# Two heads to a task for half of the kept heads, with V in 8 KB rows, in a two-layer cached decode kernel

## The chip, the cores and the metric

One core of one Trainium2 chip runs the kernel. The metric is the device time of one execution in microseconds (us), the median over the runs of a measurement. The kernel before has 1160.96 us (three runs, 1160.77 to 1161.88).

## What is computed

Two layers of grouped-query attention against a cache and a dense block with SiLU, for 8 batches of one token. The same caches and weights serve both layers.

```python
B, Sq, D = 8, 1, 512
Hq, Hkv, Sk, Dh = 32, 8, 8192, 128          # 4 query heads to each cached head
k_cache, v_cache: (B, Hkv, Sk, Dh) bf16     # 2 MB for each batch and head
...
q = (x @ wq) by heads
scores = einsum("bhqd,bhkd->bhqk", q, k) * Dh ** -0.5
o = einsum("bhqk,bhkd->bhqd", softmax(scores), v)
attention = o @ wo
dense(x) = silu(x @ w1) @ w2                # F = 1792
...
x = x + attention(layernorm(x)); x = x + dense(layernorm(x))     # layer 0
x = x + attention(layernorm(x)); x = x + dense(layernorm(x))     # layer 1
```

## The kernel before

**Tasks and positions.** A task is one (layer, batch, head): 128 tasks in an order that `make_tasks` writes out. A task has eight positions, so that the loop over `p` runs over 1024 positions and some more at the end. A head's 8192 keys are four granules `k` of 512 KB (128 partitions of 4 KB). At each position the loop emits, in this order, what is due there: the task's queries (`emit_q`), DVE transposes of K (`emit_t`), scores (`emit_s`), the product with V (`emit_pv`), the steps that join and fold the output (`emit_own`, `emit_join`, `emit_fold`), the softmax of an earlier task, one stage of a batch's chain (wo, layer norm, the dense block, the queries of layer 1), and the loads (`issue_until`). Each engine runs its instructions in that order.

**Slots.** `ARENA` has 28 slots of 4 KB in each partition. Heads 3 to 7 of a batch are kept: their K (20 slots) is loaded and transposed in layer 0 and stays for layer 1. Heads 0 to 2 load K in both layers, one granule a slot. V is loaded in both layers, one granule a slot. Kept K is loaded 2 MB at a time, in rows of 16 KB; all other K and all V in rows of 4 KB. For each batch the order is: five kept tasks of layer 0, some five tasks of heads 0 to 2 of other batches or of layer 1 (in which the chain of the batch runs), then its five kept tasks of layer 1. In the middle part kept K fills 20 slots, and eight are left.

**Loads.** `plan_loads` sorts the loads by `need`, the position at which one is used, and gives each the slot that comes free first; `after` is the position after which it may be issued. SP issues them all in that order, and waits at each for the slot's last reader. V has `need = i0 + 1 + LP` for a granule that starts at position `i0`; `LP = 14` is the distance from scores to the product with V.

**Scores and softmax.** K is transposed in place by DVE in 32x32 blocks of 32-bit words (line 497). A kept head is scored at once (line 563), 16 matmuls of 512 columns that fill one PSUM bank `SCp`. The softmax of task `p // 8 - 1` follows: DVE's maximum over the bank (574) and `top` (576), POOL's maximum over partitions (579), DVE's shift (583, 586), ACT's exp into `P` (590), the row sums (597, 599), PE's transposes of `P` (608), ACT's copy to `PT` (612). `P` shares its bytes with `E`, where the output is joined (643, 651). PV is line 628, the last fold 665, the norm 675, a wo part 780.

```python
soft = {0: [softmax_max], 2: [softmax_shift, softmax_exp], 4: [softmax_sum], 5: [emit_pt], 7: [softmax_rcp]}
```

Of the kernel before, what the change touches and what calls it, by code (L numbers as in the profile page):

```python
# [5 lines left out]
HQ = 32  # L6
DH = 128
SM_SCALE = DH ** -0.5
# [11 lines left out]
READ = (1, 1, 1, 4, 4, 4, 4, 4)  # L20
KEEP = 20
LT = 1
PRE = 10
LP = 14
EARLY = 4
DEAL_AT = 30
WO_FROM = 36
NTP = 2
NSCP = 2
NPT = 1  # L30
# [12 lines left out]
NAT = 2  # L43
CW = 32
# [98 lines left out]
class Load:  # L143


    __slots__ = ("kind", "b", "g", "k", "turn", "need", "free", "slot", "after", "wide")

    def __init__(self, kind, b, g, k, need, free, wide=1):
        self.kind, self.b, self.g, self.k, self.turn = kind, b, g, k, k
        self.need, self.free, self.wide = need, free, wide  # L150
        self.slot, self.after = None, None


def make_tasks(nb, nkv, keep_from):
# [10 lines left out]
    na = 0  # L165
    for b in range(nb):
        if b:
            tasks += kept[b]
        size = -(-(2 * first * (nb - 1)) // nb) if b in (0, nb - 1) else 2 * first * (nb - 1) // nb
        must = max(0, first * min(b + 1, nb - 1) - na)  # L170
        nd = size if b == nb - 1 else min(len(behind), first, size - must)
        tasks += behind[:nd]
        del behind[:nd]
        take = ahead[na:na + size - nd]
        na += len(take)
        tasks += take
        if b + 1 == nb:
            tasks += behind
        tasks += c[b]
        behind += d[b]  # L180
# [4 lines left out]
def plan_loads(tasks, kept, nslot, ngran):  # L185

    at = {t: i for i, t in enumerate(tasks)}
    loads = []
    for i, (layer, b, g) in enumerate(tasks):
        for k in range(ngran):  # L190
# [8 lines left out]
            loads.append(Load("V", b, g, k, i0 + GPG - 1 + LP, i0 + GPG - 1 + LP))  # L199
# [9 lines left out]
    for d in loads:  # L209
        w = ngran if d.kind == "K" and (d.g, d.k) in kept else 1  # L210
        if w > 1 and d.k:
            d.slot = whole[d.g] + d.k
            d.after = by
            assert d.after < d.need or d.need == -1 and d.after == -2, (d.kind, d.need, d.after)
            continue
# [7 lines left out]
        if w > 1:  # L223
            whole[d.g] = d.slot
# [19 lines left out]
def _build(ctx, nc, A_x, A_k_cache, A_v_cache, A_wq, A_wo, B_w1, B_w2, out):  # L244
# [43 lines left out]
    def half(slot, h):  # L288
# [8 lines left out]
    XT = [sb([128, KT, B], BF16, f"XT{n}") for n in range(3)]  # L297
# [5 lines left out]
    QT2 = [sb([128, HQ], BF16, "QT2") for _ in range(2)]  # L303
# [12 lines left out]
    hsT = sb([128, FT * B], BF16, "hsT")  # L316
    xnT = sb([128, KT, B], BF16, "xnT")
    s1 = sb([128, B], FP32, "s1")
    s1a = sb([128, B], FP32, "s1a")
    s2 = sb([128, 1], FP32, "s2")  # L320
    s2a = sb([128, 1], FP32, "s2a")
    top = sb([128, REP], FP32, "top")
    tops = sb([128, REP], FP32, "tops")
    ssm = [sb([128, REP], FP32, "ssm") for _ in range(NST)]
    ssa = [sb([128, REP], FP32, "ssa") for _ in range(NST)]
    widths = {"own_q": NQ, "hm": REP, "far": REP, "mine": REP, "own_x": XW, "real": 1, "rowmax": 1,
              "eps": 1, "shift": 1, "eh": FT, "vr": B, "yr": B, "tr": B}
    widths.update({f"rcp{n}": REP for n in range(NST)})
    widths.update({f"rs{n}": 1 for n in range(NST)})
    row = sb([128, sum(widths.values())], FP32, "row")  # L330
    tiny, at_col = {}, 0
    for name, w in widths.items():
        tiny[name] = row[:, at_col:at_col + w]
        at_col += w
    own_q, hm, far, mine, own_x, real, rowmax, eps, shift, vr, yr, tr = (
        tiny[n] for n in ("own_q", "hm", "far", "mine", "own_x", "real", "rowmax", "eps", "shift", "vr", "yr", "tr"))
    rcp = [tiny[f"rcp{n}"] for n in range(NST)]
    rs = [tiny[f"rs{n}"] for n in range(NST)]

# [56 lines left out]
    v_slot = {}  # L396

    def issue(d):
        cache = A_k_cache if d.kind == "K" else A_v_cache
        if d.kind == "K":  # L400
            src = cache[d.b, d.g].rearrange("(p k c) d -> k p (c d)", k=NGRAN // d.wide, p=128)[d.k // d.wide]
        else:
            src = cache[d.b, d.g].rearrange("(k p c) d -> k p (c d)", k=NGRAN, p=128)[d.k]
# [7 lines left out]
    with nc.Block() as block:  # L411

        @block.sync
        def _(sync_eng):
# [13 lines left out]
                    hm[:, :], lanes.rearrange("p c (k r) -> p r c k", k=NGRAN), AX.XY, ALU.add),  # L428
                reads=["ident"], writes=["hm"],
            )  # L430
            op(
# [7 lines left out]
            for n in range(NSCP):  # L439
                op(dve, lambda n=n: dve.memset(SCp[n][:, :], 0.0), writes=[f"SC{n}"])  # L440
            op(dve, lambda: dve.tensor_reduce(real[:, :], hm[:, :], AX.X, ALU.add), reads=["hm"], writes=["real"])
# [3 lines left out]
            op(dve, lambda: dve.tensor_scalar(  # L445
                far[:, :], hm[:, :], real[:, 0:1], FAR, op0=ALU.subtract, op1=ALU.mult),
               reads=["hm", "real"], writes=["far"])
# [57 lines left out]

            span_of = {}
# [10 lines left out]
            def emit_queries(layer, b):  # L517
                if layer == 0:
                    q, rq = QT1[:, b * HQ:(b + 1) * HQ], f"QT1_{b}"
                else:  # L520
                    q, rq = QT2[b % 2][:, :], f"QT2_{b % 2}"
# [9 lines left out]
            def emit_q(ti):  # L531
                layer, b, g = tasks[ti]
                if ti == span_of[(layer, b)][0]:
                    emit_queries(layer, b)
                n = ti % NQB
                at = qset[(layer, b)] * NPART * HQ
                op(dve, lambda: dve.tensor_tensor(
                    QB[n][:, :, :].rearrange("p i (a r) -> p i a r", a=NQ),
                    QSp[:, at:at + NPART * HQ].rearrange("p (i h) -> p i h", h=HQ)[:, :, g * REP:(g + 1) * REP].unsqueeze(2)
                    .to_broadcast([128, NPART, NQ, REP]),  # L540
                    own_q[:, :].unsqueeze(1).unsqueeze(3).to_broadcast([128, NPART, NQ, REP]), ALU.mult),
                   reads=["QS", "own_q"], writes=[f"QB{n}"])

            def emit_s(i):
# [9 lines left out]
                bank, qn = ti % NSCP, ti % NQB  # L554
# [17 lines left out]
            def softmax_max(ti):  # L572
                bank = ti % NSCP
                op(dve, lambda: dve.tensor_reduce(rowmax[:, :], SCp[bank][:, :], AX.X, ALU.max),  # L574
                   reads=[f"SC{bank}"], writes=["rowmax"])
                op(dve, lambda: dve.scalar_tensor_tensor(  # L576
                    top[:, :], hm[:, :], rowmax[:, 0:1], far[:, :], op0=ALU.mult, op1=ALU.add),
                   reads=["hm", "rowmax", "far"], writes=["top"])
                op(pool, lambda: pool.partition_all_reduce(tops[:, :], top[:, :], 128, bass.bass_isa.ReduceOp.max),  # L579
                   reads=["top"], writes=["tops"])  # L580

            def softmax_shift(ti):
                op(dve, lambda: dve.scalar_tensor_tensor(  # L583
                    mine[:, :], tops[:, :], -SM_SCALE, hm[:, :], op0=ALU.mult, op1=ALU.mult),
                   reads=["tops", "hm"], writes=["mine"])
                op(dve, lambda: dve.tensor_reduce(shift[:, :], mine[:, :], AX.X, ALU.add), reads=["mine"], writes=["shift"])  # L586

            def softmax_exp(ti):
                bank, st = ti % NSCP, ti % NST
                op(act, lambda: act.activation(  # L590
                    P[:, :].rearrange("p (x j k) -> p k x j", x=CPB, k=NGRAN),
                    SCp[bank][:, :].rearrange("p (k x j) -> p k x j", k=NGRAN, x=CPB), ACT.Exp, bias=shift[:, 0:1], scale=SM_SCALE, accum_out=rs[st][:, :]),
                   reads=[f"SC{bank}", "shift"], writes=["P", f"rs{st}"])

            def softmax_sum(ti):
                st = ti % NST
                op(act, lambda: act.activation(ssm[st][:, :], hm[:, :], ACT.Copy, scale=rs[st][:, 0:1]),  # L597
                   reads=["hm", f"rs{st}"], writes=[f"ssm{st}"])
                op(pool, lambda: pool.partition_all_reduce(ssa[st][:, :], ssm[st][:, :], 128, bass.bass_isa.ReduceOp.add),  # L599
                   reads=[f"ssm{st}"], writes=[f"ssa{st}"])  # L600

            def emit_pt(ti):
                pb = ti % NPT
# [494 lines left out]
```

## Time and profile before

| | |
|---|---|
| median of three runs | 1160.96 us (1160.77 to 1161.88) |
| the profiled execution | 1160.11 us, span 1158.0 us |
| busy share of the span | PE 61%, DVE 64%, ACT 29%, POOL 10% |
| granted TensorE clock | 0.605 of full speed |
| HBM read | 465.05 MB, 402 GB/s over the span |
| chain that ended last | DMA 52%, DVE 20%, issue 10%, PE 8%, SP's queue 5%, ACT 4% |
| loads of V | 512 of 512 KB, 10.7 us from issue to landing (median) |
| loads of K | 192 of 512 KB, 8.2 us; 40 of 2 MB, 19.1 us |

The page cuts the span in 40 slices; for each it gives DMA's busy share in tenths and the GB/s. Stretches of time show the busy time of each engine, the granted clock, DMA's share (it exceeds 1 where packets overlap) and the rate. In the timeline a line is: start in us, duration, engine, line of the source, operation, output and input, count, and in brackets the idle time before it and what ended it. SPq is the queue from which SP issues loads.

### The profile page before, as it was taken

What the parts mean: (1) busy time and instruction counts of PE and PEld (TensorE: products, weight loads), DVE (VectorE), ACT (ScalarE), POOL (GpSimd) and SP (SyncE); (2) the same over time, 40 slices, a digit from 0 to 9 for tenths busy, and PEclk for the clock granted to TensorE, in tenths of its full rate; (3) what the DMA queues carried; (4) which work ended last, traced back from release to release, by engine and by line L of the source; (5) the groups of instructions that cost most, each with busy time, mean ns of one, the idle gap of its engine ahead of it and who ended that gap; (6) DMA issues with size and microseconds to landing.
All of it is one profiled execution on the core that took longest, in us unless ns stands there. A gap on an engine that the chain in (4) does not pass through costs nothing.

```text
span 1158.0 us, 26486 instructions
## 1 busy us (share of the span) xinstructions
PE 703.8 (61%) x10768; PEld 343.4 (30%) x10768; DVE 740.4 (64%) x1781; ACT 337.9 (29%) x764; POOL 117.1 (10%) x296
## 2 busy tenths in 40 slices
PE   1434666556755676567655587557655676557666
PEld 1212342223321342134322342124222342134233
DVE  3646773677557675677457664777467755677564
ACT  0442234223332233222422233222323233223332
POOL 0000111001110111001100111001100111001100
PEclk9756567565655566555855565566756565565665
DMA  9999999999999999999999999999999999999994
GB/s 372 393 411 415 407 409 413 416 406 409 408 420 413 398 407 417 418 395 408 410 416 414 403 407 416 419 397 409 412 419 403 407 408 418 415 403 407 407 408 192
DMA packets 112601, 466.80 MB, mean 403 GB/s; under 512 B 11984, under 2 KB 16096, under 8 KB 106720
## 3 DMA queue, kind: packets, MB, share of 16 engines
q1 hardware_dynamic: 112480, 465.11, 100.1%
q8 instruction: 85, 1.39, 0.5%
q14 instruction: 36, 0.29, 0.1%
HBM read 465.05 MB, written 0.01 MB: 402 GB/s over the span
## 4 chain that ended last, share of the span: by engine, by line
DMA 52%; DVE 20%; issue 10%; PE 8%; SPq 5%; ACT 4%; POOL 1%; DVEq 0%; ACTq 0%; POOLq 0%
DMA arena<-in_A_k_cache_dram 32%; DMA arena<-in_A_v_cache_dram 20%; DVE E L651 7%; DVE arena L497 7%; SPq L379 5%; DVE row L574 3%; PE SCp L563 2%; PE OTp L628 2%; PE TPp L608 2%; ACT E L590 2%; ACT PT L612 1%; DVE top L576 1%; POOL tops L579 1%; ACT E L643 1%; DVE row L586 1%
## 5 line engine op out<-in xcount | busy, mean ns | idle before, releaser
L497 DVE STREAM_TRANSPOSE arena<-arena 128x1024 int32<-128x1024 int32 x352 | 434.1, 1237 | 230.3 <-DMA arena<-in_A_k_cache_dram 230.0
L590 ACT ACTIVATE E<-SCp,row 128x512 bf16<-128x512 f32 x128 | 183.0, 1429 | 655.8 <-DVE row L586 620.5
L628 PE MATMUL OTp<-arena,PT 128*16 128x512 bf16 (+1 forms) x2064 | 280.2, 557 | 130.5 <-DMA arena<-in_A_v_cache_dram 108.9
L563 PE MATMUL SCp<-arena,QB 128*16 128x128 bf16 (+1 forms) x4352 | 249.8, 373 | 112.3 <-DVE arena L497 93.3
L651 DVE SCALAR_TENSOR_TENSOR E<-OTp,row,E 128x128 f32<-128x128 f32 x381 | 130.0, 341 | 110.0 <-ACT E L643 100.9
L563 PEld LDWEIGHTS SCp<-arena,QB 128*16 128x16 bf16 x4352 | 95.1, 107 | 218.2 <-DVE arena L497 136.9
L628 PEld LDWEIGHTS OTp<-arena,PT 128*16 128x16 bf16 (+1 forms) x2064 | 56.8, 105 | 207.5 <-DMA arena<-in_A_v_cache_dram 156.0
L579 POOL PARTITION_ALL_REDUCE tops<-top x128 | 47.7, 372 | 629.5 <-DVE top L576 501.5
L608 PE MATMUL TPp<-ident,E 128*128 128x128 bf16 x512 | 72.0, 288 | 58.5 <-ACT E L590 56.0
L665 PE MATMUL OTp<-row,E 128*128 128x4 f32 x254 | 69.0, 342 | 40.0 <-DVE E L651 39.9
L665 PEld LDWEIGHTS OTp<-row,E 128*128 128x128 f32 x254 | 57.9, 284 | 107.4 <-DVE E L651 97.6
L599 POOL PARTITION_ALL_REDUCE ssa<-ssm x128 | 56.0, 438 | 319.4 <-ACT ssm L597 319.4
L574 DVE TENSOR_REDUCE row<-SCp 128x1 f32<-128x512 f32 x128 | 84.7, 661 | 0.7 <-PE SCp L563 0.7
L608 PEld LDWEIGHTS TPp<-ident,E 128*128 128x128 bf16 x512 | 40.8, 123 | 141.4 <-ACT E L590 114.2
L780 PE MATMUL MISC<-at,wo 128*128 128x32 bf16 x1024 | 37.2, 187 | 58.8 <-DVE row L583 50.0
L612 ACT COPY PT<-TPp 128x256 bf16<-128x256 bf16 x128 | 47.6, 372 | 78.5 <-PE TPp L608 78.4
L780 PEld LDWEIGHTS MISC<-at,wo 128*128 128x128 bf16 x1024 | 32.9, 105 | 65.3 <-DVE at L675 61.2
L643 ACT ACTIVATE E<-OTp,row 128x128 f32<-128x128 f32 x127 | 47.3, 372 | 0.0
L762 PE MATMUL MISC<-xnT,wq 128*128 128x32 bf16 (+1 forms) x1152 | 35.1, 183 | 18.3 <-DVE xnT L749 13.9
L762 PEld LDWEIGHTS MISC<-xnT,wq 128*128 128x128 bf16 x1152 | 33.7, 103 | 24.6 <-issue 18.0
L597 ACT ACTIVATE ssm<-row 128x4 f32<-128x4 f32 x128 | 38.1, 297 | 3.9
L590 ACT ACTIVATION_READ_ACCUMULATOR E<-SCp,row 128x1 f32 x128 | 34.1, 266 | 0.0
(100 smaller groups left out, 308.7 us busy)
## 6 DMA issues: line engine op xcount, KB each, us to landing
arena<-in_A_v_cache_dram SPq DMA_DIRECT2D x512, 512.0 KB, 10.7
arena<-in_A_k_cache_dram SPq DMA_DIRECT2D x192, 512.0 KB, 8.2
arena<-in_A_k_cache_dram SPq DMA_DIRECT2D x40, 2048.0 KB, 19.1
wq<-in_A_wq_dram SPq DMA_DIRECT2D x1, 4096.0 KB, 16.6
wo<-in_A_wo_dram SPq DMA_DIRECT2D x1, 4096.0 KB, 33.2
w<-in_B_w_dram SPq DMA_DIRECT2D x2, 1792.0 KB, 24.6
E<-in_A_x_dram SPq DMA_DIRECT2D x1, 8.0 KB
out_dram<-E SPq DMA_DIRECT2D x1, 8.0 KB
```

The costliest lines, as they stand in the source:

```text
L497: op(dve, lambda: dve.transpose(words, words), reads=[r_half(slot, 0), r_half(slot, 1)], writes=[r_half(slot, 0), r_half(slot, 1)])
L563: lambda n=n, t=t: pe.matmul(SCp[bank][t * QUAD:t * QUAD + USED, lo * 128:(lo + len(slots)) * 128], QB[qn][:, n, :], keys(t, n), start=(n ...
L574: op(dve, lambda: dve.tensor_reduce(rowmax[:, :], SCp[bank][:, :], AX.X, ALU.max), reads=[f"SC{bank}"], writes=["rowmax"])
L579: op(pool, lambda: pool.partition_all_reduce(tops[:, :], top[:, :], 128, bass.bass_isa.ReduceOp.max), reads=["top"], writes=["tops"])
L590: op(act, lambda: act.activation(P[:, :].rearrange("p (x j k) -> p k x j", x=CPB, k=NGRAN), SCp[bank][:, :].rearrange("p (k x j) -> p k x ...
L608: lambda c=c: pe.transpose(tpv[:, c, :], P[:, c * 128:(c + 1) * 128], ident[:, :])
L612: op(act, lambda: act.copy(PT[pb][:, :, :, :, :].rearrange("p a t x r -> p x t a r"), tpv.rearrange("p x (t q) -> p x t q", q=QUAD)[:, :, ...
L628: lambda t=t, y=y: pe.matmul(OTp[ob][t * QUAD:t * QUAD + w * REP, 0:w * DH], PT[pb][:, k, t, y * w:(y + 1) * w].rearrange("p x r -> p (x r)"),
L651: op(dve, lambda x=x: dve.scalar_tensor_tensor(joint, OTp[ob][:, x * DH:(x + 1) * DH], own_x[:, x:x + 1], joint, op0=ALU.mult, op1=ALU.add ...
L665: lambda: pe.matmul(OTp[ob][:, 0:REP], joint, hm[:, :], start=True, stop=True)
L762: lambda o=o, k=k: pe.matmul(MISC[:, o * n:o * n + w], w_sb[:, k, o * 128:(o + 1) * 128], rhs_of(k).to_broadcast([128, w]) if n == 1 else ...
L780: lambda o=o, h=h: pe.matmul(MISC[:, o * w:(o + 1) * w], wo_sb[:, h, o * 128:(o + 1) * 128], rhs_of(h).to_broadcast([128, w]) if n == 1 el ...
```

## The change

Heads 4 and 5, and 6 and 7, become pairs (`DUOS`). A pair's K is read as before in two loads of 2 MB with 16 KB rows, but each load has 64 partitions of one head and 64 of the other, half of each head's keys. The scores of a load go to two banks (`score_both`), 32 matmuls of 256 columns; after the second load both banks hold both heads, and one softmax serves the two: a maximum over each bank and one over the two, one `top` of 8 columns, one shift, two exps one after another through `P`, with a transpose after each (`emit_turn`), and two `PT`. V of these heads is read in rows of 8 KB, two granules a load, into two neighbouring slots, and used at once by `emit_pv`; where the planner finds a pair whose `need - after` is under 12 positions (`AMPLE`), it reads the two granules singly and plans again. To this belong: `LP` from 14 to 22, the softmax emitted one task later (`p // 8 - 2`), three `SCp` banks, one `TPp` and two `PT`, and the queries of a batch's first layer 1 task emitted at position 4 of the task (`LATE`) and not three ahead of it. To find room in SBUF, `XT`, `QT2`, `xnT`, `hsT` and small rows share bytes or become single; what they compute stays. `make_tasks` now balances the tasks of heads 0 to 2 by a due count, which moves a few of them between batches.

```diff
+DUOS = (4, 6)
+AMPLE = 12
-LP = 14
+LP = 22
-DEAL_AT = 30
-WO_FROM = 36
-NTP = 2
-NSCP = 2
-NPT = 1
+DEAL_AT = 38
+WO_FROM = 44
+NTP = 1
+NSCP = 3
+NPT = 2
+LATE = 4
...
+def lead_of(g):
+    return g - 1 if g - 1 in DUOS else g
+def members(g):
+    return 2 if lead_of(g) in DUOS else 1
...
 def plan_loads(tasks, kept, nslot, ngran):
+    apart = set()
+    while True:
+        loads = deal(tasks, kept, nslot, ngran, apart)
+        close = {d.key for d in loads if d.kind == "V" and d.wide > 1 and d.need - d.after < AMPLE}
+        if not close:
+            return loads
+        apart |= close
...
-            loads.append(Load("V", b, g, k, i0 + GPG - 1 + LP, i0 + GPG - 1 + LP))
+            key = (layer, b, g, k // members(g))
+            w = 1 if key in apart else members(g)
+            if k % w == 0:
+                loads.append(Load("V", b, g, k, i0 + GPG - 1 + LP, i0 + GPG - 1 + LP, w))
+                loads[-1].key = key
...
         if d.kind == "K":
-            src = cache[d.b, d.g].rearrange("(p k c) d -> k p (c d)", k=NGRAN // d.wide, p=128)[d.k // d.wide]
+            rows = cache[d.b, lead:lead + n].rearrange("g (p f) d -> (g p) (f d)", p=128 // n)
+            at = own if d.wide > 1 else d.k * n + own
+            src = rows[:, at * d.wide * SLOT:(at + 1) * d.wide * SLOT]
         else:
-            src = cache[d.b, d.g].rearrange("(k p c) d -> k p (c d)", k=NGRAN, p=128)[d.k]
+            rows = cache[d.b, d.g].rearrange("(k p c) d -> k p (c d)", k=NGRAN // n, p=128)[d.k // n]
+            src = rows[:, d.k % n * SLOT:(d.k % n + d.wide) * SLOT]
...
+            def score_both(ti, slots, qn):
+                own = tasks[ti][2] - lead_of(tasks[ti][2])
+                cols = NGRAN // 2 * 128
+                many = ARENA[:, slots[0] * SLOT:(slots[0] + NGRAN) * SLOT].rearrange(
+                    "p (k u t x h j e) -> p u t h e k x j", u=2, t=NQ, x=CPB, h=PAIRS, e=2, j=QUAD)
+                for u in range(2):
+                    bank = (ti - own + u) % NSCP
+                    mm_group([
+                        lambda n=n, t=t: pe.matmul(
+                            SCp[bank][t * QUAD:t * QUAD + USED, own * cols:(own + 1) * cols], QB[qn][:, n, :],
+                            many[:, u, t, n // 2, n % 2], start=(n == 0), stop=(n == NPART - 1))
+                        for n in range(NPART) for t in range(NQ)
+                    ], ...)
...
+            def softmax(ti, ph):
+                many = members(tasks[ti][2])
+                if ph == 0:
+                    softmax_max(ti)
+                elif ph == 2:
+                    softmax_shift(ti)
+                    softmax_exp(ti, 0)
+                elif ph == 3 and many > 1:
+                    emit_turn(ti, 0)
+                    softmax_exp(ti, 1)
+                elif ph == 4:
+                    softmax_sum(ti)
+                elif ph == 5:
+                    emit_turn(ti, many - 1)
+                    emit_pt(ti)
+                elif ph == 7:
+                    softmax_rcp(ti)
...
             def emit_pv(i):
+                if v_wide.get((b, g, k - k % members(g)), 1) > 1 and k % members(g):
+                    return
+                parts = [(v_slot[(b, g, k + m)], (lead + (k + m) % many) % NPT) for m in range(v_wide[(b, g, k)])]
                 steps = [
...
-                    for y in range(CPB // w) for t in range(NQ)
+                    for slot, pb in parts for y in range(CPB // w) for t in range(NQ)
                 ]
...
-                ti, ph = p // GPT - 1, p % GPT
-                if 0 <= ti < ntask and ph in soft:
-                    for f in soft[ph]:
-                        f(ti)
+                ti = p // GPT - 2
+                if 0 <= ti < ntask and lead_of(tasks[ti][2]) == tasks[ti][2]:
+                    softmax(ti, p % GPT)
```

## The prediction

> **What bounds the kernel now.** I read the page's slices and queue rows first, then the stretches of time by stage, then the order of time around one place where the DMA rate sags.
>
> ```profile
> span 1158.0 us, 26486 instructions
> ...
> DMA  9999999999999999999999999999999999999994
> GB/s 372 393 411 415 407 409 413 416 406 409 408 420 413 398 407 417 418 395 408 410 416 414 403 407 416 419 397 409 412 419 403 407 408 418 415 403 407 407 408 192
> ...
> q1 hardware_dynamic: 112480, 465.11, 100.1%
> ...
> arena<-in_A_v_cache_dram SPq DMA_DIRECT2D x512, 512.0 KB, 10.7
> arena<-in_A_k_cache_dram SPq DMA_DIRECT2D x192, 512.0 KB, 8.2
> arena<-in_A_k_cache_dram SPq DMA_DIRECT2D x40, 2048.0 KB, 19.1
> ```
>
> All 16 DMA engines are busy from the first load to the last one; PE, DVE and ACT have 61%, 64% and 29%. The last V lands at 1144.8 us (a PV that waited for it starts at 1144.85), and 13.2 us of tail follow. So the time is the length of one stream of 465.11 MB, plus a tail, as long as no engine lets the stream run dry. What can change it is the bytes (unchanged), the rate at which a row of a given length goes, and holes in the stream.
>
> The rate depends on the row length:
>
> ```profile
> core 0: us, PE busy (x) PEld busy (x) DVE busy (x) ACT busy (x) POOL busy (x), PEclk, DMA share, GB/s
> 8.00:16.00 8.00, 0.24 (x4) 0.18 (x4) 2.93 (x12) 0.00 (x0) 0.28 (x1) 1.00 1.02 424
> 130.00:190.00 60.00, 39.83 (x752) 22.59 (x752) 38.94 (x104) 19.13 (x49) 7.23 (x18) 0.64 1.03 408
> 190.00:240.00 50.00, 28.33 (x284) 10.92 (x288) 31.14 (x72) 14.19 (x30) 4.82 (x12) 0.57 1.02 419
> 292.00:316.00 24.00, 19.07 (x288) 9.08 (x288) 12.23 (x39) 8.98 (x19) 2.87 (x8) 0.64 1.03 407
> ```
>
> The first row is wq alone (8 KB rows), the second K and V in 4 KB rows, the third 16 KB K rows and 4 KB V rows half and half, the fourth V alone (4 KB rows, contiguous). At 1.02 or 1.03 all are saturated, so 424 against 408 is the row length. The trace's packet records agree: a 4 KB row holds an engine for 160 ns (median), an 8 KB row for 309, a 16 KB row for 615.
>
> **The rows: what is removed.** V of heads 4 to 7 in both layers is 64 heads of four granules, 256 loads of 512 KB. The new planner, which is arithmetic on positions and can be worked through from the source, leaves 96 pairs of 1 MB (192 granules) and reads 64 granules singly. Loads go from 744 to 648. The pairs hold 96 x 128 = 12,288 rows of 8 KB, where there were 24,576 of 4 KB: 100.7 MB change rate.
> - By the packet records: 2 x 160 - 309 = 11 ns for each pair of rows, 12,288 x 11 ns / 16 engines = 8.4 us.
> - By the stretches: 100.7 MB x (1/408 - 1/424) = 9.3 us.
> - By 4 KB and 16 KB rows, drawn as a line: (4 x 160.3 - 612.7) / 3 = 9.5 ns for each row saved (fitted over full stretches, with the completion packets in them), 7.3 us.
> I take 8.2 us, and 7.3 to 9.3 for the range.
>
> A rule of the Trainium skill sizes the same thing smaller ("DMA: Bandwidth & Descriptors", "Why small descriptors are slow (HBM only)"): about three cycles of overhead for each packet, on one beat for each 32 bytes. By it two 4 KB rows take 2 x 131 beats and one 8 KB row 259, 1.1% less, an estimate of 2.8 us on the 247 us of those rows. The trace shows 3.4% (309 against 320 ns), so I stay with the trace.
>
> **K of the pairs.** The 32 wide K loads of heads 4 to 7 keep 2 MB and 16 KB rows, but the rows now lie 32 KB apart (64 partitions from each head). K in 4 KB rows 16 KB apart goes at 408 GB/s, V in touching 4 KB rows at 407: no cost of distance up to 16 KB. I take none.
>
> **Compute, off the path.** Scores of a paired head become 32 matmuls of 256 columns for 16 of 512. A group of 16 takes 1.89 us at 512 columns and 0.61 at 128; on a line between, 2 x 1.04 = 2.07, so +0.18 us x 64 heads = 12 us on PE, hidden in its 39% idle time. For each of the 32 pairs (8 batches, 2 layers, 2 pairs) DVE saves one `top` (0.22), one shift (0.14 + 0.16) and one reciprocal (0.17), adds the join of two maxima (nearest row 0.13) and the sums that ACT did (bounded by 0.1 and 0.3): 0.3 us less. POOL does two reductions for four. Maxima, transposes, exps, PT copies and joins keep their number. None of it is on the stream.
>
> **LP from 14 to 22.** All V comes eight positions later, and the softmax is emitted at `p // 8 - 2`, so each PV stands behind its PT as before. The planner gives both versions 336 positions with only seven slots ahead of the work. At the end, 12 V granules instead of 8 follow the last K (15 us of stream, where the last softmax takes about 7 from the last K's landing to its PT: 1135.1 to 1141.9), so the last V stays last and the 13.2 us stay. At the start the 28 slots and the weights keep the queue full. Cost 0; if a start or end showed through, 1 us.
>
> **Holes in the stream.** Eight times, when kept K fills 20 slots, eight slots are left. Around seven of these entries the packet records show holes, 1.6 us of idle in all. This is one:
>
> ```profile
> 369.62 1.25 DVE L497 STREAM_TRANSPOSE arena<-arena 128x1024 int32<-128x1024 int32 x1 [3.02 <-DMA arena<-in_A_k_cache_dram]
> 371.61 0.33 SPq L379 DMA_DIRECT2D arena<-in_A_k_cache_dram  x1
> 371.87 0.66 DVE L574 TENSOR_REDUCE row<-SCp 128x1 f32<-128x512 f32 x1
> 374.05 0.61 PE L780 MATMUL MISC<-at,wo 128*128 128x32 bf16 x16 [1.53 <-DVE at L675]
> 374.59 1.03 PE L628 MATMUL OTp<-arena,PT 128*16 128x512 bf16 x8
> 375.29 0.33 SPq L379 DMA_DIRECT2D arena<-in_A_v_cache_dram  x1
> 379.11 0.33 SPq L379 DMA_DIRECT2D arena<-in_A_v_cache_dram  x1
> ```
>
> K of head 7 lands at 369.6; DVE transposes four granules with a join and a softmax between them, PE's PV waits behind a wo part that waits for the norm, and SP can issue only as slots come free. At 379.1, 11 slots had been issued behind that K and 9.5 / 1.28 = 7.4 had passed: 3.6 slots (4.6 us) of lead, and the faster engines run dry while the slowest does not.
>
> After the change the softmax of heads 6 and 7 falls into the next task, so this burst loses max and `top` (0.88 us). But pairs come free as pairs. Walking the new order with the same durations: two K at +5.4 us, then nothing until the 32 matmuls and the paired PV are through, at +9.7; then 10 slots issued less 7.6 passed leave 2.4 slots, 3.1 us. A transfer needs 1.0 us from issue to its first packet (0.79 to 1.80 at the start), so 2.1 us are spare. Then comes the double softmax: PE's first `emit_turn` waits for the first exp (1.43 + 0.27), the second exp for that turn (0.61), and the next K's score stands behind them. Its lead by the same count is 2.8 to 4.1 slots. So I take 0 for the holes, bounded by -1.6 us (they vanish) and by the rival below. LATE puts the queries of a batch's first layer 1 task one position ahead of its scores, at the end of that stage: up to 6 us of PE work against 8 slots (10.3 us). Hidden too.
>
> **Sum.** The profiled execution took 1160.11 us, 2.11 outside its span, and 0.85 below the median 1160.96. 1160.11 - 8.2 = 1151.9; for the median 1152.8.
>
> **Rivals.**
> 1. *The entries starve the stream, and it gets slower.* Place: each of the eight entries. If the two turns and the paired release come later than I walked, the spare 2.1 us are used and each further microsecond is lost eight times. It outweighs the gain from 8.2 / 8 = 1.0 us more, 3.1 us late in all; at 4 us late 8 x 1.9 = 15 us are lost, 1168. For it: lead already thin, and PE now waits for ACT in mid task. Against: 3.02 us of DVE idle ahead of each kept K, which recover lateness.
> 2. *Distance costs rate, no change.* If 16 KB rows 32 KB apart go as 4 KB rows do, 67 MB lose (1/430 - 1/408), 8.4 us (430 for 16 KB rows from 419 half and half): 1161. The Trainium skill tells of such a loss at far larger pitches ("DMA: Bandwidth & Descriptors", "Latency and other measured facts"): 103 GB/s at 4 MiB, 164 at 2 MiB, 207 at 512 KiB, where 214 is full; by it 32 KB would cost nothing. No run here has a pitch above 16 KB.
> 3. *Half the gain goes into holes*, 0.5 us at each entry: 1157.
>
> **Chances.** A measurement of this kernel can tell 0.2%, 2.3 us, from no change. Forecast 0.60, rival 3 0.10 (also faster), rival 2 and mixtures that cancel 0.08, rival 1 0.22. Faster 0.70, same 0.08, slower 0.22. Low end: 9.3 + 1.6 saved, 1150.0, and a little for the start, 1149.5; high end 1165.0, inside rival 1 at 3.6 us late, which leaves out some 0.14 above. The forecast's own range is 1150 to 1155.
>
> **What would show it.** Right: some 12,300 fewer packets on q1 and 8 KB rows near 309 ns; stretches of V of heads 4 to 7 near 420 GB/s; 16 KB rows still 615 ns; idle between first and last load not above 2 us more; the same 13 us tail. Wrong: slices under 390 GB/s at the eight entries, with SP waiting for PE scores and PE's transposes for the exp (rival 1), or longer 16 KB rows (rival 2).

## The result, and the profile after

The changed kernel takes 1174.56 us (median of four runs, 1172.0 to 1175.2) against 1160.87 us of the kernel before, a ratio of 1.0113 with an interval of 1.0095 to 1.013. The forecast was 1152.8 us. The profiled execution took 1174.63 us, with a span 14.9 us longer than before.

These are the lines of the page that answer to those shown of before: the span, DMA's busy tenths and GB/s in 40 slices, the load queue, and the loads with their median time from issue to landing.

```profile
span 1172.9 us, 28314 instructions
...
DMA  9999999999999999999999999999999999999993
GB/s 365 403 404 392 401 407 426 418 383 408 392 421 391 403 404 423 421 366 409 415 423 402 394 408 424 418 378 408 412 425 407 384 400 420 420 382 408 405 412 142
...
q1 hardware_dynamic: 98656, 465.10, 98.9%
...
arena<-in_A_v_cache_dram SPq DMA_DIRECT2D x320, 512.0 KB, 8.8
arena<-in_A_k_cache_dram SPq DMA_DIRECT2D x192, 512.0 KB, 8.2
arena<-in_A_v_cache_dram SPq DMA_DIRECT2D x96, 1024.0 KB, 14.1
arena<-in_A_k_cache_dram SPq DMA_DIRECT2D x40, 2048.0 KB, 16.2
```

The rows did what was asked of them: 13,824 fewer packets (12,288 of them rows), and slices of 420 to 426 GB/s where paired V runs. But slices of 366 to 394 stand among them, one at each of the eight entries into the stage of eight free slots. DMA's row of tenths doesn't show it. It is nine everywhere, because some packets of a starved stream last longer: the mean 4 KB packet went from 163.7 to 166.5 ns while the median fell from 160 to 159, and in the entry from 232 to 250 us one packet in a hundred takes over 507 ns, in the full stretch from 130 to 160 us over 172.

Stretches of the changed kernel, with the columns of those of before:

```profile
core 0: us, PE busy (x) PEld busy (x) DVE busy (x) ACT busy (x) POOL busy (x), PEclk, DMA share, GB/s
130.00:160.00 30.00, 18.84 (x450) 12.53 (x450) 22.00 (x54) 8.90 (x28) 4.00 (x10) 0.56 1.03 408
190.00:210.00 20.00, 13.70 (x198) 6.73 (x190) 15.83 (x33) 4.44 (x9) 0.77 (x2) 0.66 1.01 424
232.00:250.00 18.00, 11.60 (x204) 6.38 (x204) 14.21 (x28) 4.11 (x8) 0.77 (x2) 0.59 0.97 367
```

4 KB rows go at 408 as before, 16 KB K with 8 KB V at 424, and the entry behind them at 367, although PE is busy 64% and DVE 79% of it. Neither engine is busy throughout; the stream waits for slots, as the timeline below shows.

To say where time went, each stretch is priced by the rows that it moved (160.3 ns for 4 KB, 312.4 for 8 KB, 612 for 16 KB, by 16 engines: prices that fit stretches without holes; the medians of the packet records are 159, 312 and 614 in the changed kernel); what is left of its length is a hole. An entry is -6 to +24 us around the landing of head 7's K, an exit -8 to +30 us around the last single K of that stage. The tail runs from the end of the last V packet to the end of the span. A load lands in 16 pieces, one from each engine. The lead is the time from the issue of a load to the last landing of the load ahead of it: the smallest at each entry, the median of eight. Each row is of one profiled execution, in us; the last column is the measured median. Executions of one kernel differ by 1 to 7 us, so a difference of 1 or 2 us between two rows tells little by itself.

| kernel | rows | entries | exits | tail | lead | time |
|---|---|---|---|---|---|---|
| before | 1131.0 | 4.8 | 2.1 | 13.2 | 4.5 | 1160.87 |
| after | 1124.7 | 18.9 | 6.0 | 17.4 | 3.5 | 1174.56 |
| e1, V singly | 1131.0 | 5.5 | 8.1 | 18.1 | 4.9 | 1170.56 |
| e2, pair 4+5 alone | 1126.8 | 7.2 | 7.0 | 15.7 | 3.7 | 1163.92 |
| e3, pair 6+7 alone | 1128.9 | 7.5 | 5.6 | 16.7 | 4.5 | 1167.92 |
| e4, no pairs | 1131.0 | 2.3 | 8.5 | 13.9 | 4.7 | 1162.72 |
| e5, singly under 17 | 1126.3 | 8.8 | 6.2 | 17.7 | 4.4 | 1167.23 |
| e6, queries early | 1124.7 | 19.2 | 23.1 | 16.2 | 3.6 | 1189.51 |
| e7, single softmax early | 1124.7 | 19.3 | 7.3 | 13.2 | 3.6 | 1172.14 |
| e8, pairs by halves | 1131.0 | 15.3 | 6.6 | 15.8 | 3.8 | 1180.19 |
| e9, pairs 3+4, 5+6, softmax early | 1125.3 | 47.4 | 6.8 | 13.5 | -0.5 | 1200.84 |
| e10, pair 4+5, softmax early | 1126.8 | 14.8 | 5.0 | 13.2 | 2.5 | 1171.02 |
| e13, pairs 3+4, 5+6 | 1125.3 | 45.5 | 9.4 | 14.7 | -0.6 | 1203.76 |
| e14, pair 4+5, singly under 17 | 1128.4 | 6.2 | 8.2 | 15.7 | 4.7 | 1164.69 |

From before to after: rows -6.3, entries +14.1, exits +3.9, tail +4.2, the start and other places -1.0, together the 14.9 us of span. This is one entry in the changed kernel, from the timeline (start, duration, engine, line, operation, idle time ahead and what ended it):

```profile
228.56 1.88 PE L595 MATMUL SCp<-arena,QB 128*16 128x256 bf16 x32 [0.81 <-DVE arena L533]
229.01 1.25 DVE L533 STREAM_TRANSPOSE arena<-arena 128x1024 int32<-128x1024 int32 x1 [0.51 <-DMA arena<-in_A_k_cache_dram]
231.39 0.33 SPq L408 DMA_DIRECT2D arena<-in_A_v_cache_dram  x1
234.25 0.80 SPq L408 DMA_DIRECT2D arena<-in_A_k_cache_dram  x2
234.99 1.88 PE L595 MATMUL SCp<-arena,QB 128*16 128x256 bf16 x32 [0.83 <-DVE arena L533]
236.66 1.06 PE L728 MATMUL OTp<-arena,PT 128*16 128x512 bf16 x8
237.44 1.47 DVE L637 TENSOR_REDUCE row<-SCp 128x1 f32<-128x512 f32 x2
237.82 0.33 SPq L408 DMA_DIRECT2D arena<-in_A_v_cache_dram  x1
240.63 0.56 PE L890 MATMUL MISC<-at,wo 128*128 128x32 bf16 x16 [2.32 <-DVE at L777]
241.81 0.33 SPq L408 DMA_DIRECT2D arena<-in_A_k_cache_dram  x1
242.67 0.33 SPq L408 DMA_DIRECT2D arena<-in_A_v_cache_dram  x1
244.61 0.61 PE L684 MATMUL TPp<-ident,E 128*128 128x128 bf16 x4 [0.96 <-ACT E L659]
246.16 0.60 PE L623 MATMUL SCp<-arena,QB 128*16 128x128 bf16 x16 [0.94 <-DVE arena L533]
246.87 0.33 SPq L408 DMA_DIRECT2D arena<-in_A_k_cache_dram  x1
```

K of head 7 lands at 229.0. SP issues one V pair, two K granules at 234.25, and then little until the 32 matmuls of 234.99 and the paired PV of 236.66 give slots back (237.82). The next gap ends at 241.81, behind the double maximum on DVE (237.44) and the wo part that waits for DVE (240.63), the third at 246.87, behind the turn that waits for the exp (244.61). These three gaps, 3.1 to 3.2 us from issue to issue, are no longer than in the kernel before (3.7 and 3.4 us in the entry that the prediction shows); what is new is that they meet a queue with 1.0 us less in it (the lead, 3.5 for 4.5). The load issued at 242.67 had a lead of 3.9 us; its first piece landed at 246.9, its last at 249.5, 2.9 us after the landing ahead of it, where a full stream takes 1.28.

### The profile page after: what moved, and what is told of

Its sections match the earlier page's. It is cut to its first block, busy times and chain, and to the rows that moved or that the text cites. A ratio compares the mean times of both kernels' runs of the same rounds, so it can differ in the third digit from the quotient of the medians.

```text
span 1172.9 us, 28314 instructions
## 1 busy us (share of the span) xinstructions
PE 697.3 (59%) x11792; PEld 380.0 (32%) x11792; DVE 738.9 (63%) x1719; ACT 315.0 (27%) x700; POOL 90.7 (8%) x232
## 4 chain that ended last, share of the span: by engine, by line
DMA 38%; DVE 19%; PE 17%; issue 14%; ACT 6%; SPq 3%; POOL 2%; DVEq 0%; POOLq 0%; ACTq 0%
DMA arena<-in_A_k_cache_dram 36%; DVE E L753 7%; DVE arena L533 4%; PE OTp L728 4%; ACT E L659 4%; PE SCp L595 3%; DVE row L637 3%; SPq L408 3%; PE TPp L684 3%; PE MISC L872 2%; DMA arena<-in_A_v_cache_dram 2%; PE SCp L623 2%; PE MISC L890 1%; ACT PT L691 1%; PE OTp L767 1%
## 5 line engine op out<-in xcount | busy, mean ns | idle before, releaser
L659 ACT ACTIVATE E<-SCp,row 128x512 bf16<-128x512 f32 x128 | 180.6, 1411 | 533.2 <-DVE row L655 454.1
L728 PE MATMUL OTp<-arena,PT 128*16 128x512 bf16 (+1 forms) x2064 | 270.0, 566 | 47.5 <-DMA arena<-in_A_v_cache_dram 27.3
L623 PE MATMUL SCp<-arena,QB 128*16 128x128 bf16 (+1 forms) x3328 | 135.7, 308 | 116.0 <-DVE arena L533 103.4
L595 PE MATMUL SCp<-arena,QB 128*16 128x256 bf16 x2048 | 116.2, 395 | 46.0 <-DVE arena L533 29.3
L623 PEld LDWEIGHTS SCp<-arena,QB 128*16 128x16 bf16 x3328 | 68.5, 108 | 182.3 <-DVE arena L533 150.1
L595 PEld LDWEIGHTS SCp<-arena,QB 128*16 128x16 bf16 x2048 | 61.4, 118 | 98.7 <-DVE arena L533 46.1
L745 ACT ACTIVATE E<-OTp,row 128x128 f32<-128x128 f32 x127 | 47.4, 373 | 164.9 <-PE OTp L728 164.9
L646 POOL PARTITION_ALL_REDUCE row<-row x96 | 36.0, 375 | 696.5 <-DVE row L643 585.1
L691 ACT COPY PT<-TPp 128x256 bf16<-128x256 bf16 x128 | 44.3, 372 | 84.7 <-PE TPp L684 84.7
L675 POOL PARTITION_ALL_REDUCE row<-row x96 | 41.3, 430 | 297.3 <-ACT row L669 140.3
L672 DVE SCALAR_TENSOR_TENSOR row<-row 128x8 f32<-128x8 f32 x32 | 7.3, 228 | 88.9 <-ACT E L659 88.9
## 6 DMA issues: line engine op xcount, KB each, us to landing
arena<-in_A_v_cache_dram SPq DMA_DIRECT2D x96, 1024.0 KB, 14.1
arena<-in_A_k_cache_dram SPq DMA_DIRECT2D x40, 2048.0 KB, 16.2
```

The costliest lines, as they stand in the source:

```text
L595: lambda n=n, t=t: pe.matmul(SCp[bank][t * QUAD:t * QUAD + USED, own * cols:(own + 1) * cols], QB[qn][:, n, :], many[:, u, t, n // 2, n % ...
L623: lambda n=n, t=t: pe.matmul(SCp[bank][t * QUAD:t * QUAD + USED, lo * 128:(lo + len(slots)) * 128], QB[qn][:, n, :], keys(t, n), start=(n ...
L659: op(act, lambda: act.activation(P[:, :].rearrange("p (x j k) -> p k x j", x=CPB, k=NGRAN), SCp[bank][:, :].rearrange("p (k x j) -> p k x ...
L691: op(act, lambda: act.copy(PT[pb][:, :, :, :, :].rearrange("p a t x r -> p x t a r"), tpv.rearrange("p x (t q) -> p x t q", q=QUAD)[:, :, ...
L728: lambda t=t, y=y, slot=slot, pb=pb: pe.matmul(OTp[ob][t * QUAD:t * QUAD + w * REP, 0:w * DH], PT[pb][:, at, t, y * w:(y + 1) * w].rearran ...
L745: op(act, lambda: act.activation(joint, OTp[ob][:, 0:DH], ACT.Copy, scale=own_x[:, 0:1]), reads=[f"OT{ob}", "own_x"], writes=["P"])
```

## The experiments

The theories: *release* (a pair gives its two slots back at once, so the lead at the entries gets too thin; this is the prediction's first rival), *softmax* (the double softmax holds PE and DVE in the burst), *distance* (V eight positions later and the softmax one task later are the cause by themselves), and *tail* (the softmax one task later leaves more work behind the last load).

**e1: V singly in every case, all else kept.**

```diff
-AMPLE = 12
+AMPLE = 99
```

> The changed kernel with AMPLE at 99: every V granule is read singly in 4 KB rows (halves of the 8 KB rows), all else of the change stays. Three theories. Softmax: the double softmax of heads 6 and 7 in the first task with eight slots holds up the scores that free slots; then the holes stay and the shorter rows cost 6 to 8 us on top: 1180 to 1183. Release: loads into pairs of slots are issued later and thin the lead; then the holes at the entries go and about 1165 to 1168 is left (the tail stays 4.3 us longer). Distance: V eight positions later and softmax one task later are the cause; then as the first, 1180 to 1183.

Measured 1170.56, ratio 1.0084 (1.0069 to 1.0099). The holes at the entries fall from 18.9 to 5.5 and the lead rises from 3.5 to 4.9 us: the paired V loads are what starves the entries. The time is nearest to the release theory, but above its 1165 to 1168. The rows' 6.3 us are given back, and the exits (8.1) and the tail (18.1) are still long, so the kernel stays slower than before without one paired V load.

**e2, e3, e4: one pair of heads, the other, none** (LP, the later softmax, LATE and the banks stay).

```diff
-DUOS = (4, 6)
+DUOS = (4,)     # e2
+DUOS = (6,)     # e3
+DUOS = ()       # e4
```

> The changed kernel with DUOS = (4,): only heads 4 and 5 are a pair, 6 and 7 are single tasks; 64 pairs of V are left of 96 (two thirds of the row gain, 4 to 5 us). Softmax: no double softmax falls into the stage with eight slots, so the holes at the entries shrink to those of the kernel before: 1160.9 - 4.5 + 4.3 (tail) + some 3 at the end of that stage = 1161 to 1164. Release: most pairs stay, so holes stay: 1170 to 1175. Distance: 1176 and more.

> The changed kernel with DUOS = (6,): only heads 6 and 7 are a pair; 32 pairs of V are left, all of layer 1. Softmax: the holes at the entries stay whole and two thirds of the row gain go: 1178 to 1180. Release: most pairs go, and with them most holes: 1164 to 1168. Distance: 1177 to 1180.

> The changed kernel with DUOS = (): no pair at all, all V in 4 KB rows touching, all tasks single; LP = 22, the softmax one task later, the queries one position before the first scores of layer 1, and all sharing of small tiles stay. Softmax and release alike: holes at the entries as in the kernel before, the tail 4.3 us longer, some 3 us at the end of the eight-slot stage: 1165 to 1169. Distance: holes stay, 1176 to 1182.

Measured 1163.92 (1.0027, 1.0017 to 1.0036), 1167.92 (1.0067, 1.0044 to 1.009) and 1162.72 (1.0017, 1.0008 to 1.0026). The entries have 7.2, 7.5 and 2.3 us: each pair alone adds about 5, both together 16.6, so the costs more than add. By its time e2 fits the softmax theory and e3 the release theory, so neither theory alone explains both. The distance theory is out: e4 keeps the later V and the later softmax, and its entries lose nothing more. With no pairs at all the entries are better than before (2.3 against 4.8), but the exits lose 8.5 (the time, 1162.72, is below every forecast). So what came with the pairs (LP 22, the later softmax, LATE) has a price of its own at the exits.

**e5: pairs only where the plan gives 17 positions** (72 pairs for 96).

```diff
-AMPLE = 12
+AMPLE = 17
```

> The changed kernel with AMPLE = 17: the three pairs of a batch that are in flight at the entry to the eight-slot stage (need - after of 12 to 16) are read singly, 72 pairs stay. Theory of the paired release: the 13.4 us of holes at the entries that single V took away go here too, and 24 pairs fewer cost 1.6 us: 1174.6 - 13.4 + 1.6 = 1162.8, with the tail and the exits as they are. Theory that pairs cost wherever they are: a quarter goes, 1172.

Measured 1167.23 (1.0059, 1.0039 to 1.008). Without the 24 tightest pairs the entries go from 18.9 to 8.8 us and the rows lose 1.6: 7.3 us are won by reading less in long rows. The release theory asked for 13.4 us at the entries and a time of 1162.8; 10.1 came.

**e6: the queries of a batch's first layer 1 task three positions ahead**, as in the kernel before.

```diff
-LATE = 4
+LATE = -3
```

> The changed kernel with LATE = -3: the queries of a batch's first layer 1 task are emitted three positions ahead of the task, as for every other task. If they cause the holes at the end of the eight-slot stage, these shrink from 6.0 us to the 2.1 of the kernel before: 1170.5. If the greater distance LP makes them, the chain has less room and they grow: 1175 to 1180.

Measured 1189.51 (1.025, 1.0233 to 1.0266). Exits go from 6.0 to 23.1 us, more than either theory had, and the entries stay. The smallest lead at an exit was 5.8 to 6.8 us before, has a median of 4.1 in the changed kernel, and is 1.1 to 1.7 in five of the eight exits here. With LP 22 the late queries are needed.

**e7: the softmax of single heads one task earlier**, as in the kernel before; pairs as changed.

```diff
-NST = 2
+NST = 3
...
-                ti = p // GPT - 2
-                if 0 <= ti < ntask and lead_of(tasks[ti][2]) == tasks[ti][2]:
-                    softmax(ti, p % GPT)
+                for back in (2, 1):
+                    ti = p // GPT - back
+                    if 0 <= ti < ntask and lead_of(tasks[ti][2]) == tasks[ti][2] and members(tasks[ti][2]) == back:
+                        softmax(ti, p % GPT)
```

> The changed kernel with the softmax of single tasks at p // 8 - 1 again (pairs stay at - 2, three sets of row sums). If the last two softmaxes one behind the other make the tail 17.5 us, it goes back to 13.2: 1170.3. Entries and exits: within 2 us of the change, since the double softmax and the pairs stay. If the tail has another cause, 1174.

Measured 1172.14 (1.0096, 1.0079 to 1.0112). The tail goes back to 13.2 us: the later softmax is needed for the longer tail, 4.2 us. It does not make it alone, since e4 has it too and a tail of 13.9. Of the 4.2 us the time kept 2.4 (1170.3 was expected); exits and entries lost 1.7 more.

**e8: each pair by two loads of 512 KB in 4 KB rows**, with the same two slots at the same positions.

```diff
-        dst = ARENA[:, d.slot * SLOT:(d.slot + d.wide) * SLOT]
-        dma(sp, dst, src, slsem[d.slot], ...)
+        if d.kind == "V" and d.wide > 1:
+            for m in range(d.wide):
+                dma(sp, ARENA[:, (d.slot + m) * SLOT:(d.slot + m + 1) * SLOT], src[:, m * SLOT:(m + 1) * SLOT], ...)
+        else:
+            ...
```

> The changed kernel with each pair of V read by two loads of 512 KB (halves of the 8 KB rows, so rows of 4 KB) into the same two slots at the same positions, and used at once as before. If the holes come from where the planner can place and free a pair, they stay and the rows cost 6.3 us more: 1180 to 1181. If they come from the 1 MB transfer itself (it lands as one), they shrink: 1165 to 1171.

Measured 1180.19 (1.0166, 1.0135 to 1.0198), 5.6 us above the changed kernel, where the rows give back 6.3. The profiled execution was the fastest of the four (1176.17 to 1183.36); its entries lose 15.3 us for 18.9. So, as the first theory expected, most of the loss remains with transfers of 512 KB: it comes from the slots that are planned and released as pairs, not from the 1 MB transfer.

**e9 and e10: the parts that looked best put together.** e9 takes heads 3+4 and 5+6 as pairs, pairs under 17 positions singly and the early single softmax; e10 takes the pair 4+5 alone with the early single softmax.

```diff
-DUOS = (4, 6)
-AMPLE = 12
+DUOS = (3, 5)   # e9, and the edit of e7
+AMPLE = 17      # e9
+DUOS = (4,)     # e10, and the edit of e7
```

> Pairs are heads 3 and 4, 5 and 6; head 7 stays single, so the double softmax falls into the task of head 7, ahead of the eight-slot stage. AMPLE = 17 (88 pairs), and the softmax of single tasks one task earlier, as in the run with the early softmax. If double softmax and pairs at the entry are the whole cause, entries come to 5 us or less, the tail to 13.3, the rows save 5.8: 1160.4 - 5.8 + 5 (exits) = 1157 to 1161. If the pairs cost wherever they are, 1165 and more.

> Only heads 4 and 5 are a pair (64 pairs of V, none read singly), and single tasks have their softmax one task earlier. The run with the one pair gave 1163.9 with a tail of 16.0 us; with the tail at 13.3 this gives 1161.2, the entries (7.2 us of holes) and exits (7.0) as there. A version that beats the kernel before only if the earlier softmax helps the exits too.

Both missed: 1200.84 (1.0349, 1.0333 to 1.0364) and 1171.02 (1.0097, 1.008 to 1.0114). In e10 the tail is repaired (15.7 to 13.2) but the entries double (7.2 to 14.8) and the lead falls from 3.7 to 2.5 us. The likely reason, not shown alone, is that with this pair the later softmax keeps the burst after head 7's K short; for this split the short tail was not had without longer entries.

**e11 and e12: the kernel before with one and two slots less.** Everything is as in the kernel before, except that the planner has 27 and 26 slots (the second line lets it skip the slots that are not there).

```diff
-NSLOT = 28
+NSLOT = 27      # e11; 26 in e12
...
-        return sorted((free[m] for m in range(q, q + ngran) if not s <= m < s + w), reverse=True)
+        return sorted((free[m] for m in range(q, q + ngran) if m in free and not s <= m < s + w), reverse=True)
```

> The kernel before with 27 slots instead of 28: seven are left in the eight-slot stage, so each transfer of it is issued 1.28 us later against the stream. This measures the lead that a transfer needs. If about 1.0 us is enough, as the prediction took it (the lead there is near 7 us), nothing is lost in the even part of the stage. If the lead must be near 5 us, as the holes after the change look, the even part loses little at 27 and much at 26. The planner also places some kept K later, so only the even part tells.

> The kernel before with 26 slots: six are left in the eight-slot stage, the lead is 2.6 us shorter than with 28, near 4.4 us. Need of 1.0 us: the even part of the stage keeps 408 GB/s. Need near 5 us: its rate falls below 400 GB/s throughout, and the time rises by 10 us and more.

One run each: 1188.79 and 1217.86, so the first slot costs 28.3 us and the second 29.1. By stage the two are not alike. Holes in us, summed over the eight passes; the stage of eight free slots is entry, middle and exit:

| kernel | loading kept K | entries | middle | exits | lead |
|---|---|---|---|---|---|
| before | 1.5 | 4.8 | 1.9 | 2.1 | 4.5 |
| e11 | 21.7 | 8.5 | 5.6 | 3.2 | 3.4 |
| e12 | 15.7 | 20.3 | 20.7 | 11.5 | 2.3 |

With 27 slots the thin stage loses 8.5 us more, and 20.2 us go ahead of it, where K of the kept heads is loaded, 3.8 to 4.5 us in each of the last five passes. The planner puts such a 2 MB load into four slots side by side that start at a multiple of four: 28 slots have seven such places, 27 and 26 have six. SP issues in the planner's order, so one load without a place holds up all behind it. In e11, ahead of the entry at 506 us, SP issues nothing from 469.8 to 484.35:

```profile
459.49 0.89 SPq L379 DMA_DIRECT2D arena<-in_A_k_cache_dram  x1
460.43 9.35 SPq L379 DMA_DIRECT2D arena<-in_A_v_cache_dram  x4
484.35 0.33 SPq L379 DMA_DIRECT2D arena<-in_A_k_cache_dram  x1
```

That the missing place is the cause is argued from the planner's code. With 26 slots the thin stage itself loses 43.7 us more. The rates by slice of e11, then of e12:

```profile
GB/s 362 392 412 393 396 403 414 417 393 409 410 417 406 405 401 416 361 394 397 414 402 362 398 404 415 363 405 400 411 406 359 402 393 416 353 407 408 407 408 207
```

```profile
GB/s 369 388 420 374 374 382 416 419 380 380 396 418 337 369 377 411 417 355 366 391 417 352 379 381 418 418 372 378 409 416 332 371 371 415 419 375 388 389 408 210
```

The fourth to sixth slices, the thin stage of the first pass, have 407 to 415 in the kernel before, 393 to 403 with 27 slots and 374 to 382 with 26, with no other edit. This is what was expected if a load needs a lead near 5 us: little lost with 27 slots, much with 26. The kernel before stands near the edge of the reserve that its stream needs.

**e13 and e14: what e9 left open.** e13 is e9 with the softmax as late as in the changed kernel; e14 is e2 with pairs under 17 positions read singly (40 pairs for 64).

```diff
-DUOS = (4, 6)
-AMPLE = 12
+DUOS = (3, 5)   # e13
+DUOS = (4,)     # e14
+AMPLE = 17      # both
```

> Pairs are heads 3+4 and 5+6, head 7 alone, V singly under 17 positions (88 pairs), as in e9, but each softmax is emitted two tasks later as in the changed kernel (p // 8 - 2). It differs from e9 in the time of the single softmaxes alone. Theory A (e9's 47 us of holes come from the single softmax emitted a task earlier, which falls onto head 7's transposes): entries go down to the 7 to 9 us of the kernels with one pair, 1163 to 1168. Theory B (they come from the double softmax of heads 5+6, which falls into head 7's task, ahead of its transposes and scores, in this order of softmaxes too): entries stay at 40 us and more, 1190 to 1202.

> Heads 4+5 alone are a pair, and V is read singly where a pair has under 17 positions (40 pairs in place of 64). Release theory: entries go from 7.2 us down to the 2.3 us of the kernel with no pairs, rows give up 1.6 us, exits and tail stay: 1161 to 1163. If the entries of e2 come from the double softmax alone: 7.2 us stay, 1165 to 1166.

e13 measured 1203.76 (1.0375, 1.036 to 1.0391) with 45.5 us at the entries, as theory B had it: the earlier softmax was not the cause of e9. Its timeline around the entry at 233.4:

```profile
232.41 0.33 SPq L408 DMA_DIRECT2D arena<-in_A_v_cache_dram  x1
232.78 0.43 SPq L408 DMA_DIRECT2D arena<-in_A_k_cache_dram  x1
235.63 1.48 DVE L637 TENSOR_REDUCE row<-SCp 128x1 f32<-128x512 f32 x2
238.82 0.61 PE L890 MATMUL MISC<-at,wo 128*128 128x32 bf16 x16 [2.67 <-DVE at L777]
240.06 0.33 SPq L408 DMA_DIRECT2D arena<-in_A_v_cache_dram  x1
244.26 1.89 PE L623 MATMUL SCp<-arena,QB 128*16 128x512 bf16 x16 [0.94 <-DVE arena L533]
```

The double softmax of heads 5+6 now stands among head 7's transposes (its maxima at 235.63), head 7 is scored 10.8 us after its K landed (6.0 in the changed kernel, 7.1 in the entry shown of before), and SP issues nothing from 232.78 to 240.06: the load behind that has a lead of -0.6 us. That the double softmax, and not another part of this split, makes the gap is argued from this order, not shown alone.

e14 measured 1164.69 (1.0036, 1.0023 to 1.0048), not below e2 and between what the two theories gave. The lead recovers (3.7 to 4.7) but the holes hardly do (7.2 to 6.2): with one pair the release seems the smaller part, and what holds the rest is open. No version beats the kernel before.

## Why the prediction was wrong

**The rows: right, a little too large.** 8.2 us were taken, 6.3 came. The term that was too large is the price of an 8 KB row: 312 ns in the changed kernel, where 309 was taken from the few rows of this length before. 320.6 - 312.4 = 8.2 ns, by 12,288 / 16. This is 2.6% of two 4 KB rows; by the Trainium skill's three cycles for a packet ("DMA: Bandwidth & Descriptors", "Why small descriptors are slow (HBM only)") it was the 1.1% estimated before. The trace stays above that rule.

**Rival 2, distance: did not happen.** 16 KB rows 32 KB apart took 614 ns (median), against 615 before.

**PE's dearer scores: hidden, as said.** 2048 matmuls of 256 columns took 116.2 us, 1.82 for a group of 32 where 2.07 was taken.

**The holes: the step that failed.** The walk of the entry was right: two K at +5.4 were forecast and came at +5.3, the paired PV's slots at +9.7 came at +8.8, and 3.1 us of lead were forecast where 3.5 was the median. What failed is the sentence after it: "A transfer needs 1.0 us from issue to its first packet (0.79 to 1.80 at the start), so 2.1 us are spare." The time to a first packet is not what a stream on 16 engines needs. The table gives what it needs: with a lead of 4.4 us and more an entry loses 0.3 to 1.1 us, at 3.4 to 3.8 it loses 0.9 to 2.4, at 2.3 to 2.5 it loses 1.9 to 2.5, at -0.5 nearly 6. So there was nothing spare. What also counts is how many loads are thin: at the eight entries 22 loads of the changed kernel have a lead under 4.5 us, 5 in the kernel before, none in e1 and 1 in e4. Over the loads of all sixteen traces, from the 41st of each on, the price of a thin lead is gradual. The time by which a load's 16 pieces land late on average, beyond the price of its rows behind the load ahead, is:

| lead, us | 6 to 7 | 5.5 to 6 | 5 to 5.5 | 4.5 to 5 | 4 to 4.5 | 3 to 4 | 2 to 3 | below 0 |
|---|---|---|---|---|---|---|---|---|
| late, us | 0.02 | 0.04 | 0.08 | 0.13 | 0.24 | 0.33 | 0.71 | 3.4 |

Rival 1 happened, with its place (each of eight entries) and about its size (14.1 us where it gave 15), but without the lateness that it asked for. Its break-even of "3.1 us late in all" should have been none, and its chance of 0.22 was too small for that reason.

The row that could have told it was in the prediction: the entry of before, with the same walk, had a lead of 4.6 us (5.1 by the landings) and already showed holes. The prediction counted 1.6 us of idle in all at these entries; by the rows' price they lose 4.8. A lead that loses a little is a measurement of the need; the 1.0 us was not. How the 14.1 us divide between the paired release and the double softmax is only known in part: with V singly the release goes and the double softmax stays (e1, 5.5 us), without pairs both go (e4, 2.3). The 3 us between these two, of one execution each, do not settle the softmax's part.

**LP from 14 to 22 at cost 0: failed twice.** First the tail, "the 13.2 us stay". The lines of the end:

```profile
1148.55 1.39 ACT L659 ACTIVATE E<-SCp,row 128x512 bf16<-128x512 f32 x1 [3.10 <-DVE row L655]
1154.38 1.41 ACT L659 ACTIVATE E<-SCp,row 128x512 bf16<-128x512 f32 x1 [3.10 <-DVE row L655]
1157.02 1.02 PE L728 MATMUL OTp<-arena,PT 128*8 128x256 bf16 x16 [0.55 <-ACT PT L691]
1159.80 1.02 PE L728 MATMUL OTp<-arena,PT 128*8 128x256 bf16 x16
```

The last V packet ends at 1155.5, but its PVs start at 1157.02 and 1159.80: the first waits for `PT`, which waits for the last exp at 1154.38, and that comes 5.83 us after the exp of the task ahead. Both stand behind the landing of the last K (1140.7) in series, and the chain is each time maximum, POOL, shift, exp. The last V packet ends 14.8 us after that landing, as forecast (15); what failed is "the last softmax takes about 7 from the last K's landing to its PT". It takes 16.2 us.

The later softmax alone does not bring it there. From the last K's landing to the end of its `PT` it is 6.8 us before, 12.6 in e4 (later softmax, no pairs, tail 13.9), 16.2 after, and 7.5 in e7 (pairs, early softmax, tail 13.2). In e4 the 12.6 us are still under the 14.8 of the V stream. There DVE waits for the last K:

```profile
1133.14 1.25 DVE L533 STREAM_TRANSPOSE arena<-arena 128x1024 int32<-128x1024 int32 x1 [1.31 <-DMA arena<-in_A_k_cache_dram]
```

In the changed kernel DVE transposes it 2.4 us after it landed: with the pairs the engines run behind the stream at the end. Which part of the pairs' work puts them there was not separated.

Second the exits, +3.9 us, which the sum had hidden in full with LATE. e4 has them without any pair (8.5), e6 shows that LATE's place is worth 17 us there. The lead says why: 5.8 to 6.8 us before, 3.0 to 4.7 in seven of e4's eight exits. Which part of what came with the pairs takes it was not separated.

## What to carry to other kernels

Ahead of a change that frees buffers in larger pieces, measure the lead of the loads (from issue to the last landing of the load ahead) in the thinnest stage, and how much the stream already loses there; a stage that loses anything has no reserve, and every microsecond of lead taken is paid at each pass. A busy share of nine tenths does not show it, GB/s by slice and packets that grow longer do. Running the unchanged kernel with one buffer less prices the reserve ahead of any rewrite, if the loss is read by stage: of the 28 us of the first slot only 8.5 were the thin stage, and the rest is put down to a planner that had lost a place for its large loads.

## What the runs showed of the hardware

A stream on 16 engines starts to lose when a load is issued with a lead under some 5.5 us (the averages above: 0.02 us late at 6 to 7 us, 0.13 at 4.5 to 5, 0.33 at 3 to 4), more than four loads of 1.28 us. Two things in the records of landings go into it. A load of 512 KB issued onto a short queue lands its first piece 2.9 to 4.2 us after issue (237.8 to 240.7 and 242.7 to 246.9 in the changed kernel, with leads of 3.7 and 3.9 us), and 2.7 us after issue where the queue had run dry (e13, 246.66 to 249.36). And the 16 pieces of a load land over 1.5 to 3.1 us at the entry shown, so that the foremost engines are through with the load ahead long before its last landing. The Trainium skill gives some 0.6 us to the first byte on this path and up to 2 us of HBM latency at high load ("DMA: Bandwidth & Descriptors", "Latency and other measured facts"); the two and the transfer's own 1.28 make 3.9 us, an estimate that lies among these landings. What part each has is not shown here.

In the stage of eight free slots one slot less of 28 costs the unchanged kernel 8.5 us, two cost 43.7 (one run each).
